# Sparse attention and expert layer on one core: routing moved on chip, tokens scattered straight from attention

## The chip, the cores and the metric

The kernel runs on one NeuronCore of a Trainium2 chip. The metric is device time in microseconds (us): 551.54 us for the kernel before (median of 3 runs, 551.34 to 552.23).

## The reference, cut to what matters

```
P = sinkhorn(sort_net)                       # 5 rounds, 8x8 per (batch, head)
k_sorted, v_sorted = P @ blocks(k), P @ blocks(v)      # blocks of 96 tokens
attn = softmax(q_blk @ k_sorted_blk.T / 8); x = attn @ v_sorted_blk   # B=4, H=8, S=768, D=64
x = x.transpose(0, 2, 1, 3).reshape(3072, 512)
logits = x @ w_gate + modality_bias[modality_id]       # 8 experts
e_idx = argmax(logits); gate_w = softmax(logits)[e_idx]
for e in range(8):                           # F = 1024
    out[e_idx == e] = gate_w * (relu(x[e_idx == e] @ w1[e]) @ w2[e])
```

Each token goes to one expert. The inputs are one fixed draw. x has a standard deviation of 0.0036, so the modality bias decides: modality 1 has its largest bias at expert 0 (0.722), modality 0 at expert 3 (0.643). The reference sends 1513 tokens to expert 0, 1559 to expert 3 and none to the others. In tiles of 128 tokens that is 12 + 13 = 25.

## The kernel before, in words

**Attention** (lines 113 to 342). k and v are sorted by matmuls with the block-diagonal P (`sort_k`, `sort_v`), batches 0 and 1 first (group 0), batches 2 and 3 (group 1) inside the loop. The loop has 32 units: unit u is one head h = u % 8 of half hf (four of the eight blocks) of two batches. A unit runs `scores` (PE), `expo` (ACT), `av` (PE, then a reciprocal and a multiply on DVE, L260 and L261) and, ahead, the next heads' query transposes (`prep_q`: a spread on DVE, six transposes on PE, a copy on DVE). The order up to line 343 is the order in which the code is written; each engine works its queue in order. POOL issues the loads of k, v, q and the weights on one DMA queue; these convert fp32 to bf16. After a head group ends, SP writes x to `x_scratch` in DRAM (L269).

**Gating** (L364 to L398): 24 tiles of 128 tokens are read back, transposed, multiplied by `w_gate`; one-hot, gate and rank within the tile stay on chip, and the counts go through DRAM.

**Placing** (L400 to L468): counts become expert bases, in matmuls of a few rows and four round trips through DRAM; then 24 indirect DMAs on POOL scatter (row number, gate) pairs to `sidx_scratch` (L465).

**Experts** (L474 to L515): 31 tiles, enough for any routing. Each loads its expert number into registers, its 128 indices (SP), gathers 128 rows of x (POOL, L481), transposes them (L487), runs the first layer (L493, 8 matmuls of 512 columns) with relu (L498, L500), transposes the result (L504, L505), runs the second layer (L508), scales (L512) and scatters 128 rows to the output (L513). All eight experts' weights lie in `w_all`, and the matmuls address it by register.

## Time and profile before

| stage of the profiled execution | from, us | to, us |
|---|---|---|
| first sort | 0 | 43.5 |
| 32 attention units | 43.5 | 122.7 |
| gating, first load of x to last count | 122.7 | 215 |
| bases and indices | 215 | 233.4 |
| 24 scatters of pairs | 233.4 | 332.8 |
| 31 expert tiles and the end | 332.8 | 553.4 |

The profiled execution took 555.13 us, with a span of 553.4 us from the first to the last instruction. Busy time over that span: PE 268.7 us (49%), DVE 199.5, POOL 153.7, ACT 143.7. HBM was read 59.83 MB. A span is read stage by stage: the engine that is busy on average need not be the one that a stage waits for.

### The profile page before, as it was taken

To read this page: it belongs to the slowest core of one execution; us is meant where nothing else is said; L and a number is where in the kernel's file an instruction comes from. 1 tells how busy PE (TensorE), PEld (TensorE's weight loads), DVE (VectorE), ACT (ScalarE), POOL (GpSimd) and SP (SyncE) were. 2 spreads that over 40 slices of the span, in tenths; PEclk is the share of its full clock that TensorE was granted. 3 is DMA by queue.
4 is the path that set the end of the run, shared out by engine and by line. 5 is a ranking of instruction groups with operands and counts; after the bars stand their busy time and mean duration, and the time that the engine had idled before them with its cause. 6 is when DMAs were issued, how large, how long until landed. Compare 5 with 4: busy or idle time off the path is not lost.

```text
span 553.4 us, 6871 instructions
## 1 busy us (share of the span) xinstructions
PE 268.7 (49%) x2044; PEld 153.5 (28%) x2044; DVE 199.5 (36%) x735; ACT 143.7 (26%) x445; POOL 153.7 (28%) x182
## 2 busy tenths in 40 slices
PE   0274696570233552000000004877887787887884
PEld 0264575440112331000000002333333333333331
DVE  7756456580233554100000001343344433433342
ACT  1142496240123552000000001333333323332331
POOL 9607414020101222222222222232232323323321
PEclk9999996555555555555555555999999989998998
DMA  6939999999994310000000001111111111111110
GB/s 129 210 62 157 66 216 222 222 221 235 224 227 81 59 43 1 8 0 0 0 0 0 0 0 29 49 57 59 58 58 55 58 58 58 64 53 58 31 22 1
DMA packets 40473, 43.56 MB, mean 79 GB/s; under 512 B 14300, under 2 KB 32773, under 8 KB 40182
## 3 DMA queue, kind: packets, MB, share of 16 engines
q0 software_dynamic: 24320, 36.72, 33.8%
q1 hardware_dynamic: 12662, 3.26, 3.6%
q10 hardware_dynamic: 3456, 3.15, 2.5%
q8 instruction: 18, 0.29, 0.2%
q14 instruction: 17, 0.14, 0.1%
HBM read 59.83 MB, written 11.33 MB: 129 GB/s over the span
## 4 chain that ended last, share of the span: by engine, by line
DMA 31%; PE 30%; issue 20%; DVE 12%; POOL 4%; ACT 2%; POOLq 0%; SPq 0%; ACTq 0%; DVEq 0%
DMA sidx_scratch<-rg_all,dest_i_all 14%; PE h_p L493 10%; PE y_p L508 9%; DMA q_in<-in_q_dram 4%; PE hT_p L504 4%; DVE y_sb L512 3%; DMA x_t<-x_scratch,idxg 3%; DMA out_dram<-y_sb,idxg 2%; POOL cnt_scratch L398 2%; DMA x_t<-x_scratch 2%; PE ka L185 2%; PE xT_p L487 1%; DMA v_sb<-in_k_dram 1%; PE va L193 1%; DVE w_all L261 1%
## 5 line engine op out<-in xcount | busy, mean ns | idle before, releaser
L487 PE MATMUL xT_p<-ident,x_t 128*128 128x128 bf16 x124 | 21.2, 221 | 139.8 <-DMA x_t<-x_scratch,idxg 121.9
L508 PE MATMUL y_p<-w_all,hT 128*128 x248 | 75.2, 376 | 0.0
L493 PE MATMUL h_p<-w_all,xT 128*128 x248 | 63.3, 401 | 8.9 <-issue 8.7
L481 POOL DMA_INDIRECT x_t<-x_scratch,idxg x31 | 30.1, 972 | 130.2 <-DMA idxg<-sidx_scratch 40.3
L488 ACT COPY xT<-xT_p 128x128 bf16<-128x128 bf16 x62 | 16.4, 265 | 165.8 <-PE xT_p L487 165.8
L504 PE MATMUL hT_p<-ident,h_sb 128*128 128x128 bf16 x248 | 49.4, 220 | 10.3 <-DVE hT L505 9.6
L488 DVE COPY xT<-xT_p 128x128 bf16<-128x128 bf16 x62 | 11.4, 217 | 109.7 <-PE xT_p L487 109.7
L487 PEld LDWEIGHTS <-x_t 128*128 128x128 bf16 x124 | 10.2, 97 | 141.9 <-DMA x_t<-x_scratch,idxg 124.3
L505 DVE COPY hT<-hT_p 128x128 bf16<-128x128 bf16 x124 | 27.9, 225 | 47.2 <-PE hT_p L504 44.5
L465 POOL DMA_INDIRECT sidx_scratch<-rg_all,dest_i_all x24 | 23.3, 973 | 77.1 <-DMA sidx_scratch<-rg_all,dest_i_all 72.9
L505 ACT COPY hT<-hT_p 128x128 bf16<-128x128 bf16 x124 | 32.7, 264 | 29.7 <-PE hT_p L504 26.9
L513 POOL DMA_INDIRECT out_dram<-y_sb,idxg x31 | 31.4, 1012 | 27.3 <-DVE xT L488 12.5
L498 DVE TENSOR_SCALAR h_sb<-h_p 128x512 bf16<-128x512 f32 x31 | 21.4, 692 | 48.4 <-PE h_p L493 46.8
L493 PEld LDWEIGHTS <-xT 128*128 128x128 bf16 x248 | 25.0, 101 | 47.6 <-issue 27.8
L508 PEld LDWEIGHTS <-hT 128*128 128x128 bf16 x248 | 23.8, 96 | 43.9 <-issue 15.7
L500 ACT ACTIVATE h_sb<-h_p 128x512 bf16<-128x512 f32 x31 | 18.5, 597 | 65.4 <-PE h_p L493 58.5
L371 PE MATMUL xT_p<-ident,x_t 128*128 128x128 bf16 x96 | 19.9, 278 | 27.5 <-ACT xT L372 14.6
L512 DVE TENSOR_SCALAR y_sb<-y_p,idxg 128x512 f32<-128x512 f32 x31 | 23.3, 751 | 27.2 <-PE y_p L508 27.2
L243 ACT ACTIVATE attnT<-sc 96x768 bf16<-96x768 f32 x32 | 26.2, 825 | 21.6 <-PE sc L237 21.6
L398 POOL DMA_DIRECT2D cnt_scratch<-cnt_sb x24 | 12.1, 504 | 58.0 <-ACT cnt_sb L397 41.0
L261 DVE TENSOR_TENSOR w_all<-op,rs 96x256 bf16<-96x256 f32 x64 | 26.9, 421 | 2.3
L504 PEld LDWEIGHTS <-h_sb 128*128 128x128 bf16 x248 | 20.6, 97 | 15.5 <-DVE h_sb L498 14.4
(128 smaller groups left out, 397.6 us busy)
## 6 DMA issues: line engine op xcount, KB each, us to landing
w_all<-in_moe_w_dram POOLq DMA_DIRECT2D x16, 1024.0 KB, 20.8
v_sb<-in_k_dram POOLq DMA_DIRECT2D x6, 512.0 KB
w_all<-in_v_dram POOLq DMA_DIRECT2D x2, 1536.0 KB, 14.6
q_in<-in_q_dram POOLq DMA_DIRECT2D x16, 192.0 KB, 13.0
x_scratch<-w_all SPq DMA_DIRECT2D x48, 64.0 KB, 5.7
x_t<-x_scratch ACTq DMA_DIRECT2D x24, 128.0 KB, 2.7
idxg<-sidx_scratch SPq DMA_DIRECT2D x31, 1.0 KB, 1.7
x_t<-x_scratch,idxg POOLq DMA_INDIRECT x31
```

The source lines that it names most:

```text
L243: nc.scalar.activation(attnT[u % 3][:, 0:8 * BLK].rearrange("p (r f) -> p r f", r=2), sc_tiles.pop(u)[0:BLK, :, 0:4 * BLK], ACT.Exp, scale ...
L261: nc.vector.tensor_tensor(xb[:, par, :, h], op[0:BLK, :, 0:D], rs.broadcast_to([BLK, 4, D]), ALU.mult)
L465: nc.gpsimd.indirect_dma_start(out=sidx_dram, out_offset=bass.IndirectOffsetOnAxis(ap=dest_i_all[:, t:t + 1], axis=0), in_=rg_all[:, t], i ...
L481: nc.gpsimd.indirect_dma_start(out=x_t, out_offset=None, in_=x_dram, in_offset=bass.IndirectOffsetOnAxis(ap=idx[:, :1], axis=0))
L487: nc.tensor.transpose(xT_p, x_t[:, c * 128:(c + 1) * 128], ident)
L488: (nc.scalar.copy if c % 2 else nc.vector.tensor_copy)(xT[:, c], xT_p)
L493: nc.tensor.matmul(h_p, xT[:, c], w_all[:, bass.ds(e_sv * WCOL + c * F + half * 512, 512)], start=(c == 0), stop=(c == 3))
L504: nc.tensor.transpose(hT_p, h_sb[:, fc * 128:(fc + 1) * 128], ident)
L505: (nc.scalar.copy if fc % 2 else nc.vector.tensor_copy)(hT[:, fc], hT_p)
L508: nc.tensor.matmul(y_p, hT[:, fc], w_all[:, bass.ds(e_sv * WCOL + 4 * F + fc * Dm, Dm)], start=(fc == 0), stop=(fc == 7))
L512: nc.vector.tensor_scalar(y_sb, y_p, gate_t[:, 0:1], None, ALU.mult)
L513: nc.gpsimd.indirect_dma_start(out=out, out_offset=bass.IndirectOffsetOnAxis(ap=idx[:, :1], axis=0), in_=y_sb, in_offset=None, bounds_chec ...
```

## The change

The tokens are handled in four quarters m of 768 (one half hf of one group, eight units). Each token gets a row of 516 bf16 in the attention buffer `xb`: 512 values, its token number and its gate.

- **Gating inside the attention loop.** While quarter m + 1 is in attention, quarter m is transposed from `xb` on PE (`gate_T`, eight 96x128 transposes, four times a quarter) and multiplied by `w_gate` (`gate_L`). `choose` makes the one-hot, `place` ranks the tokens with ten matmuls, the running counts staying on chip, and scatters eight blocks of 96 whole rows from `xb` into `xs_scratch`, which has a region of 3200 rows per expert. The fourth quarter's gating is done in tiles 0 to 6.
- **Weights only if used.** `load_w` reads a flag into a POOL register and issues the two halves of an expert's weights under that condition: experts 0 to 3 after quarter 0, all eight after quarter 2 and after quarter 3, each only if the expert is newly used. In this draw experts 0 and 3 are loaded in the first step; the other 18 calls have a false flag.
- **Tiles from tables.** After quarter 2 a table names expert and first row of 11 full tiles; after quarter 3 another does for the rest. A tile's rows come by a plain SP load at a register address, six buffers deep (`x_load`). 25 tiles always run; tiles 25 to 30 stand under conditions that are false in this draw. The tile loop is written as a pipeline: first layer of tile s, row transposes of s + 1, second layer of s - 1, hidden transposes of s, with one copy for four transposes. The scale moves from DVE to ACT. Zero rows are written behind each expert's last row (`pad_fill`).
- Gone are `x_scratch`, `sidx_scratch` and the passes of counts through DRAM, the filling of `sidx_scratch`, and the gathers. The modality numbers are loaded at the start in six DMAs of 4-byte elements.

```diff
-    for t in range(NT):
-        r0 = t * 128
-        x_t = mpool.tile([128, Dm], BF16)
-        nc.scalar.dma_start(out=x_t, in_=x_dram[r0:r0 + 128])
...
-        nc.gpsimd.dma_start(out=cnt_dram[t:t + 1], in_=cnt_sb)
...
-    for t in range(NT):
-        nc.gpsimd.indirect_dma_start(
-            out=sidx_dram,
-            out_offset=bass.IndirectOffsetOnAxis(ap=dest_i_all[:, t:t + 1], axis=0),
-            in_=rg_all[:, t], in_offset=None)
...
-    for s in range(NS):
-        e_sv = nc.values_load(slote_sb[0:1, s:s + 1], min_val=0, max_val=7)
-        idxg = mpool.tile([128, 2], I32)
-        nc.sync.dma_start(out=idxg, in_=sidx_dram[s * 128:(s + 1) * 128])
...
+    GW = Dm + 4
+    NTL = N // BLK
+    CAP = N + 128
+    S1, SU, SMAX = 11, 25, 31
...
+    xs_dram = nc.dram_tensor("xs_scratch", [E * CAP + 128, GW // 2], I32, kind="Internal").ap()
...
+    for e in range(1, E):
+        nc.gpsimd.memset(ebase[0:1, :, e:e + 1], float(CAP * e))
...
+    def gate_T(m, c):
+        tp = mipsum.tile([128, 8, BLK], BF16, tag="mi", name=f"gt{m}_{c}")
+        for t in range(8):
+            nc.tensor.transpose(tp[:, t], xb[m % 2][:, t, c * 128:(c + 1) * 128], ident[:BLK, :BLK])
+        (nc.scalar.copy if m == 2 else nc.vector.tensor_copy)(xTg_buf(m, c), tp)
...
+    def gate_L(m, c):
+        lg = mipsum.tile([BLK, 8, E], FP32, tag="mi", name=f"lg{m}_{c}")
+        for t in range(8):
+            nc.tensor.matmul(lg[:, t], xTg_buf(m, c)[:, t], wg_sb[:, c], start=True, stop=True)
...
+            nc.vector.tensor_tensor(la, la, lg, ALU.add)
...
+        mx = small.tile([BLK, 8, 1], FP32, tag="mx", name=f"mx{m}")
+        nc.vector.tensor_reduce(mx, la, AX.X, ALU.max)
+        ls = small.tile([BLK, 8, E], FP32, tag="ls", name=f"ls{m}")
+        nc.vector.tensor_tensor(ls, la, mx.broadcast_to([BLK, 8, E]), ALU.subtract)
+        key = small.tile([BLK, 8, E], FP32, tag="key", name=f"key{m}")
+        tw = bass.AP(tensor=tiew.tensor, offset=tiew.offset, ap=[tiew.ap[0], [0, 8], tiew.ap[1]])
+        nc.vector.scalar_tensor_tensor(key, ls, 0.0, tw, ALU.is_ge, ALU.mult)
...
+        nc.tensor.matmul(rkf, maskUT[0:BLK, :], oh.rearrange("p t e -> p (t e)"), start=True, stop=False,
+                         skip_group_check=True)
+        nc.tensor.matmul(rkf, ones_bf[0:BLK, :], ebase.rearrange("p t e -> p (t e)"), start=False, stop=False,
+                         skip_group_check=True)
+        nc.tensor.matmul(rk, ones_bf[0:BLK, :], pb, start=False, stop=False, skip_group_check=True)
+        for t in range(7):
+            ob = bass.AP(tensor=oh.tensor, offset=oh[:, t].offset, ap=[oh.ap[0], [0, 7 - t], [1, E]])
+            nc.tensor.matmul(rk[:, t + 1:8], ones_bf[0:BLK, :], ob, start=False, stop=(t == 6),
+                             skip_group_check=True)
...
+        nc.vector.tensor_tensor(sel_r, rk[0:BLK], oh, ALU.mult)
+        dest = small.tile([BLK, 8], I32, tag="dest", name=f"dest{m}")
...
+        scat[m] = []
+        for t in range(8):
+            nc.gpsimd.tensor_copy(icol[:, t:t + 1], idm[:, t // 4, t % 4:t % 4 + 1])
+            ins = nc.gpsimd.indirect_dma_start(
+                out=xs_dram, out_offset=bass.IndirectOffsetOnAxis(ap=dest[:, t:t + 1], axis=0),
+                in_=xt.bitcast(I32)[:, t], in_offset=None)
+            tc.declare_no_dep(ins.ins, group="xs", reason="scattered rows are disjoint")
+            tc.add_to_no_dep_group("xs", ins.ins)
+            scat[m].append(ins.ins)
...
+        nc.tensor.matmul(cp, ones_bf[0:BLK, :], ohs[(m + 1) % 2], start=True, stop=True)
...
+            nc.vector.scalar_tensor_tensor(fI, cnt[cm][0:1], 0.0, p, ALU.is_gt, ALU.subtract)
...
+    def load_w(st, e):
+        v_ = nc.values_load(flags[st][0:1, e:e + 1], engines=(PoolEng,), min_val=0, max_val=1)
+        w1v = w_all[:, e * WCOL:e * WCOL + 4 * F].rearrange("p (c f) -> p c f", c=4)
+        w2v = w_all[:, e * WCOL + 4 * F:(e + 1) * WCOL].rearrange("p (c f) -> p c f", c=8)
+        i1 = nc.gpsimd.dma_start(out=w1v, in_=moe_w1[e].rearrange("(c p) f -> p c f", p=128), cond=v_ > 0)
+        i2 = nc.gpsimd.dma_start(out=w2v, in_=moe_w2[e].rearrange("(c p) f -> p c f", p=128), cond=v_ > 0)
+        w_dma[st] += [i1.ins, i2.ins]
...
+    def pad_fill():
+        for e in range(E):
+            row = nc.values_load(prow[0:1, e:e + 1], engines=(SPEng,), min_val=0, max_val=E * CAP - 128)
+            ins = nc.sync.dma_start(out=xs_dram[bass.ds(row, 128)], in_=zrow.bitcast(I32))
...
+    def x_load(s, after=()):
+        tb, n = slot_tab(s)
+        row = nc.values_load(tb[0:1, 1, n:n + 1], engines=(SPEng,), min_val=0, max_val=E * CAP)
+        ins = nc.sync.dma_start(out=xt_b[s % XB].bitcast(I32), in_=xs_dram[bass.ds(row, 128)])
+        for a in after:
+            tc.add_manual_dep(ins.ins, a.name, SYNC, reason="rows of the slot")
...
+    def mX(s):
+        tp = mipsum.tile([128, 4, 128], BF16, tag="mi", name=f"mx{s}")
+        for c in range(4):
+            nc.tensor.transpose(tp[:, c], xt_b[s % XB][:, c * 128:(c + 1) * 128], ident)
+        nc.vector.tensor_copy(xT_b[s % 3], tp)
...
+    def mL1(s):
+        tb, n = slot_tab(s)
+        ev = nc.values_load(tb[0:1, 0, n:n + 1], engines=(PEng,), min_val=0, max_val=(E - 1) * WCOL)
+        hp = scpsum.tile([128, 2, 512], FP32, tag="sc", name=f"hp{s}")
+        for half in range(2):
+            for c in range(4):
+                w_mm(s, hp[:, half], xT_b[s % 3][:, c],
+                     w_all[:, bass.ds(ev + (c * F + half * 512), 512)], start=(c == 0), stop=(c == 3))
+            hd = h_b[s % 2][:, half * 512:(half + 1) * 512]
+            if half == 0:
+                nc.vector.tensor_scalar(hd, hp[:, half], 0.0, None, ALU.max)
+            else:
+                nc.scalar.activation(hd, hp[:, half], ACT.Relu)
+        st_["ev", s] = ev
...
+    def mH(s):
+        for z in range(2):
+            tp = mipsum.tile([128, 4, 128], BF16, tag="mi", name=f"ht{s}_{z}")
+            for c in range(4):
+                fc = z * 4 + c
+                nc.tensor.transpose(tp[:, c], h_b[s % 2][:, fc * 128:(fc + 1) * 128], ident)
+            (nc.scalar.copy if z else nc.vector.tensor_copy)(hT_b[s % 2][:, z * 4:(z + 1) * 4], tp)
...
+    def mL2(s):
+        ev = st_.pop(("ev", s))
+        yp = opsum.tile([128, Dm], FP32, tag="op", name=f"yp{s}")
+        for fc in range(8):
+            w_mm(s, yp, hT_b[s % 2][:, fc],
+                 w_all[:, bass.ds(ev + (4 * F + fc * Dm), Dm)], start=(fc == 0), stop=(fc == 7))
+        xt = xt_b[s % XB]
+        y = y_b[s % YB]
+        nc.scalar.activation(y, yp, ACT.Copy, scale=xt.bitcast(FP32)[:, Dm // 2 + 1:Dm // 2 + 2])
+        idc = xt.bitcast(I32)[:, Dm // 2:Dm // 2 + 1]
+        ix = small.tile([128, 1], I32, tag="ix", name=f"ix{s}", bufs=4)
...
+            nc.gpsimd.tensor_tensor(ix, idc, keep2[:, s - S1:s - S1 + 1], ALU.mult)
+            nc.gpsimd.tensor_tensor(ix, ix, pen2[:, s - S1:s - S1 + 1], ALU.add)
+        else:
+            nc.gpsimd.tensor_copy(ix, idc)
+        ins = nc.gpsimd.indirect_dma_start(
+            out=out, out_offset=bass.IndirectOffsetOnAxis(ap=ix, axis=0),
+            in_=y, in_offset=None, bounds_check=N - 1, oob_is_err=False)
...
+    for m in range(4):
+        for c in range(4):
+            at(8 * m + 2 * c + 2, gate_T, m, c)
+            at(8 * m + 2 * c + 3, gate_L, m, c)
+        if m < 3:
+            at(8 * m + 9, choose, m)
+            at(8 * m + 10, place, m)
+            if m == 0:
+                at(11, counts, 0)
+                at(11, make_flags, 1)
+                for e in range(EH):
+                    at(12, load_w, 1, e)
+            if m == 2:
+                at(27, counts, 2)
+                at(27, t1_a)
+                at(28, t1_b)
+                at(28, make_flags, 2)
+                at(29, t1_c)
+                for e in range(EH):
+                    at(29, load_w, 2, e)
...
+    nc.gpsimd.memset(zrow, 0.0)
+    nc.sync.dma_start(out=xs_dram[E * CAP:E * CAP + 128], in_=zrow.bitcast(I32))
+    for e in range(EH, E):
+        load_w(2, e)
+    for s in range(XB):
+        x_load(s, scat[0] + scat[1] + scat[2] if s == 0 else ())
...
+    def load3():
+        make_flags(3)
+        for e in range(E):
+            load_w(3, e)
...
+    hooks = {(0, 0): [(gate_T, (3, 3))], (1, 0): [(gate_L, (3, 3)), (choose, (3,))],
+             (1, 1): [(place, (3,))], (2, 0): [(counts, (3,))], (3, 0): [(t2_a, ()), (pad_table, ())], (5, 2): [(pad_fill, ())],
+             (4, 0): [(t2_b, ())], (5, 0): [(t2_c, ())], (6, 1): [(load3, ())]}
...
+    def run(sl, pre=()):
+        mX(sl[0])
+        for s in sl:
+            mL1(s)
+            for f, a in hooks.get((s, 0), []):
+                f(*a)
+            if s + 1 in sl:
+                mX(s + 1)
+            if s - 1 in sl:
+                mL2(s - 1)
+            for f, a in hooks.get((s, 1), []):
+                f(*a)
+            if s + XB - 1 < SU and s >= 1:
+                x_load(s + XB - 1, scat[3] if s + XB - 1 == S1 else ())
+            for f, a in hooks.get((s, 2), []):
+                f(*a)
+            mH(s)
+        mL2(sl[-1])
...
+    n2 = nc.values_load(nT2[0:1, 0:1], min_val=0, max_val=S2)
+    rest = ExitStack()
+    for s in range(SU, SMAX):
+        rest.enter_context(tc.If(n2 > s - S1))
```

The first place is POOL in units 8 to 16 of the attention loop, where weights and queries share POOL's queue. In the kernel before (`w_all<-in_moe_w_dram` is one half of an expert's weights, `q_in` the queries of two heads):

```order
L280 DMA w_all<-in_moe_w_dram 128x8x512
L278 DMA w_all<-in_moe_w_dram 128x4x1024
L102 DMA q_in_2_986<-in_q_dram 128x2x384 x2
L280 DMA w_all<-in_moe_w_dram 128x8x512
L102 DMA q_in_3_1027<-in_q_dram 128x2x384 x2
```

In the changed kernel (`ubuf<-in_q_dram` are queries, `xs_scratch<-xb` is a scattered row block, `fl` holds the flags; the pair of the first two rows stands eight times, the weight rows four times):

```order
L413 COPY xb_77<-idI 96x1
L414 DMA xs_scratch<-xb_77,dest_1084 25728x258
...
L448 TENSOR_LOAD fl_1162
L448 ISA x2
L451 ISA
L451 DMA w_all<-in_moe_w_dram 128x4x1024
L452 ISA
L452 DMA w_all<-in_moe_w_dram 128x8x512
...
L121 DMA ubuf<-in_q_dram 128x2x384 x4
```

The last query loads of the second group, which stood between single weight loads, now stand behind eight scatters and four pairs of weight loads.

The second place is SP between tiles 5 and 11 of the expert phase, the changed kernel alone (`prow` holds the ends of the experts' regions; before, SP had one plain load per tile there, `idxg<-sidx_scratch`). In brackets is what a row waits for; DMAHW with a number is one lane of SP's DMA completions:

```order
L577 TENSOR_LOAD prow [waits DVE_49]
L577 ISA x2
L578 ISA
L578 DMA xs_scratch<-v_sb_73 128x258 [waits DMAHW3_49,DMAHW4_49,DMAHW2_49,DMAHW7_49,DMAHW1_49,DMAHW0_49]
L577 TENSOR_LOAD prow
L577 ISA x2
L578 ISA
L578 DMA xs_scratch<-v_sb_73 128x258 [waits DMAHW5_49]
...
L585 TENSOR_LOAD tab_463 [waits DVE_49]
L585 ISA x2
L586 ISA
L586 DMA v_sb_73<-xs_scratch 128x258 [waits DMAHW4_49,Activation_49,Pool_49]
```

Eight writes of zero rows, each waiting for the one before it (the next lane), now stand ahead of the load of tile 11's rows.

The third place is PE inside one tile. Before, transposes of the hidden layer and the second layer's matmuls alternate:

```order
L504 LDWEIGHTS h_sb
L504 MATMUL hT_p<-ident,h_sb 128x128
L508 LDWEIGHTS hT
L508 ISA
L508 MATMUL y_p<-w_all,hT 128x512
L504 LDWEIGHTS h_sb
```

Now (`yp` is the second layer of the tile before, `ht` the transposed hidden layer of this tile, `hp` the first layer of the next):

```order
L599 MATMUL yp_2670<-w_all,ubuf 128x512
L625 LDWEIGHTS ubuf
L625 MATMUL ht_0_2696<-ident,ubuf 128x128
...
L625 MATMUL ht_1_2702<-ident,ubuf 128x128
L607 TENSOR_LOAD tab_462
L607 ISA x2
L599 LDWEIGHTS ubuf
L599 ISA
L599 MATMUL hp_2718<-w_all,ubuf 128x512
```

The eight second-layer matmuls now stand in a block between the first layer and the transposes that it feeds, so another tile's work lies between a result and its use.

599 lines of the change are left out of this document (323 added, 276 removed).

## The prediction, made before the result was known

> **What bounds the kernel now.** I read the granted clock over the 40 slices first, then the busy times stage by stage, then the chain of waits. Clock, in tenths of full speed:
>
> ```profile
> PEclk9999996555555555555555555999999989998998
> ```
>
> The stages (from:to and length in us; busy us and instructions of PE, PEld, DVE, ACT, POOL; granted clock; DMA share; GB/s):
>
> ```profile
> 0.00:43.50 43.50, 14.57 (x162) 12.69 (x162) 30.38 (x68) 10.79 (x20) 22.85 (x28) 1.00 0.66 128
> 43.50:122.70 79.20, 55.16 (x768) 44.96 (x768) 51.42 (x164) 39.20 (x60) 28.43 (x34) 0.78 1.18 188
> 122.70:145.40 22.70, 0.42 (x3) 0.26 (x4) 0.44 (x4) 0.18 (x1) 1.76 (x4) 0.50 1.17 231
> 145.40:233.40 88.00, 31.45 (x244) 18.74 (x243) 35.54 (x254) 28.95 (x147) 15.78 (x32) 0.50 0.44 82
> 233.40:332.80 99.40, 0.00 (x0) 0.00 (x0) 0.00 (x0) 0.00 (x0) 23.34 (x24) 0.50 0.01 0
> 332.80:543.40 210.60, 164.13 (x852) 75.55 (x852) 80.04 (x243) 63.02 (x212) 60.54 (x61) 0.96 0.16 50
> ```
>
> Between 122.7 and 332.8 us, 210 us, PE is busy for 32 us: that is the routing. The last 99 us hold nothing but 24 POOL instructions. The chain (start, length, what) says what they wait for, and shows one steady expert tile:
>
> ```profile
> 45.08 12.26 DMA q_in<-in_q_dram
> ...
> 93.15 12.38 DMA q_in<-in_q_dram
> ...
> 233.47 3.85 DMA sidx_scratch<-rg_all,dest_i_all
> ...
> 328.74 4.06 DMA sidx_scratch<-rg_all,dest_i_all
> ...
> 339.38 0.76 issue
> 340.14 3.57 PE h_p L493 x8
> ...
> 398.78 0.75 DVE y_sb L512
> ...
> 399.93 0.28 issue
> 400.21 1.89 PE h_p L493 x8
> 402.09 0.28 PE hT_p L504 x2
> ...
> 405.23 0.75 DVE y_sb L512
> ```
>
> Each scatter waits until the one before it has landed, about 4 us. The first layer of the first tile starts at 339.38 + 0.76 = 340.1. A tile takes 405.23 - 398.78 = 6.45 us. Attention waits for queries twice, 12 us each, because these share POOL's queue with other loads. Three stages therefore carry the change: attention (does it grow?), the way from its end to the first tile, and the tile's cadence.
>
> **The change part by part: attention.** An ACT exponential marks each unit; the five below are units 3, 10, 18, 22 and 31.
>
> ```profile
> 60.42 0.81 ACT L243 ACTIVATE attnT<-sc 96x768 bf16<-96x768 f32 x1
> 77.94 0.85 ACT L243 ACTIVATE attnT<-sc 96x768 bf16<-96x768 f32 x1
> 94.02 0.81 ACT L243 ACTIVATE attnT<-sc 96x768 bf16<-96x768 f32 x1 [1.80 <-PE sc L237]
> 108.12 0.81 ACT L243 ACTIVATE attnT<-sc 96x768 bf16<-96x768 f32 x1 [5.94 <-PE sc L237]
> 120.06 0.81 ACT L243 ACTIVATE attnT<-sc 96x768 bf16<-96x768 f32 x1 [0.44 <-PE sc L237]
> ```
>
> Prices of kinds of work (busy us, mean ns; what ended the idle time before):
>
> ```profile
> L221 DVE COPY w_all<-tq 128x768 bf16<-128x768 bf16 x16 | 8.9, 555 | 6.2 <-PE tq L218 6.1
> L260 DVE RECIPROCAL rs<-op 96x4 f32<-96x4 f32 x64 | 11.0, 172 | 11.0 <-PE op L257 10.7
> L261 DVE TENSOR_TENSOR w_all<-op,rs 96x256 bf16<-96x256 f32 x64 | 26.9, 421 | 2.3
> L382 DVE TENSOR_REDUCE stats<-logits 128x1 f32<-128x8 f32 x24 | 3.7, 154 | 0.2
> L451 DVE TENSOR_TENSOR tmp_all<-rank_all,basebc_all 128x192 f32<-128x192 f32 x1 | 0.4, 358 | 6.6 <-DMA basebc_all<-base_scratch 6.6
> L280 POOL DMA_DIRECT2D w_all<-in_moe_w_dram x8 | 7.2, 894 | 40.5 <-PE op L257 27.1 <-DMA modraw<-in_moe_modality_id_dram 13.4
> L328 POOL MEMSET v_sb<- 128x128 bf16 x1 | 0.7, 653 | 0.1
> L465 POOL DMA_INDIRECT sidx_scratch<-rg_all,dest_i_all x24 | 23.3, 973 | 77.1 <-DMA sidx_scratch<-rg_all,dest_i_all 72.9 <-DVE dest_i_all L458 4.2
> ```
>
> And the transfers (KB each, median us from issue to landing):
>
> ```profile
> w_all<-in_moe_w_dram POOLq DMA_DIRECT2D x16, 1024.0 KB, 20.8
> q_in<-in_q_dram POOLq DMA_DIRECT2D x16, 192.0 KB, 13.0
> x_scratch<-w_all SPq DMA_DIRECT2D x48, 64.0 KB, 5.7
> x_t<-x_scratch ACTq DMA_DIRECT2D x24, 128.0 KB, 2.7
> cnt_scratch<-cnt_sb POOLq DMA_DIRECT2D x24, 0.0 KB, 1.6
> ```
>
> Up to unit 3 I change nothing: the new iotas on POOL and the modality loads delay DVE by some us, but that unit waits for queries till 57.3 (first chain row) anyway. If they delayed those queries too, the cost would be the same few us. Units 3 to 10 took 77.94 - 60.42 = 17.5. Now the transposes and logits of quarter 0 stand among them, a DVE copy of 0.56 or a small add of 0.16 per unit; taken as 0.5 each, 3.5 in all (0 if DVE's gaps take them, 5 with PE's part on top). Unit 10 starts at about 81.5. There `place` adds about 2.5, then POOL issues eight scatters at 0.97 plus a small copy and gaps, 1.3 each: done at 94.5. No scatter waits for the landing of another now. Then four expert calls, two of them real: four halves at 0.9, four flag reads at 0.76 and two skipped issues, about 8.2, so POOL comes to the last four query loads at 102.7 (the kernel before: issued by 93). One MB half takes 1.05 MB / 0.22 = 4.7 us at the 219 to 231 GB/s of the rows, so the queries stand behind 4 x 4.7 = 18.8 us of weights begun at 96, plus 3.5 of their own: they land near 118.5. The unit that needs them, 18, was 16.1 after unit 10; with gating 22.5, it is ready at 104. **The wait** is 15 us (0 if transfers issued late overtake, 23 if the weights take their median 20.8 twice). Units 18 to 23 at 2.25 end near 132.
>
> Units 24 to 31: DVE has 16 pairs of L260 and L261 (9.5 us), three copies (1.7), and 40 small operations of quarters 2 and 3 and of the first table, 37 at 0.16 and three at 0.36 (7.0): 18.2 us, or 2.3 a unit. PE is cold there as before:
>
> ```profile
> 110.00:120.00 10.00, 9.48 (x131) 6.35 (x132) 9.03 (x33) 6.45 (x8) 1.64 (x2) 0.50 1.18 219
> ```
>
> These 10 us have PE busy for 9.48 and DVE for 9.03, at 1.33 us a unit ((120.06 - 108.12) / 9), and the clock stays at 0.50. With gating matmuls on that PE I take 2.6 a unit, 21 us, and 2 for the end: **attention ends near 155** instead of 122.7 (bounds 137, no wait and 1.9 a unit, and 165). The Trainium skill, page "TensorE: Matmul & The Clock Gate", section "What's actually happening", says that some 3.4 us of sustained activity bring the full clock; this row has three times that at half clock. By the rule these units would be bound by DVE alone, 2.3 each, 2.4 us less in all.
>
> **From attention to the first tile.** The last scatter of quarter 2 leaves POOL at about 152. Four skipped expert calls follow. No row shows a skipped load. Its lower bound is one exposed register load with its issue, 0.76 (the row at 339.38); the upper adds two full DMA issues, 0.76 + 2 x 0.89 = 2.5. I take 1.6, the middle: 158.4. Then POOL clears the zero rows (0.7), SP writes them (1.6 to 5.7; 2.3 taken, as the queue is empty by then) and loads tile 0 (2.7), whose transposes and copy follow in 0.8 (L504 below, L221): 164.9. The other four skipped calls run beside this until 165. First layer at **165**, against 340.1: 175 us come from here. What is late next is only quarter 3, which the tiles hide.
>
> **The tiles.** Durations of a first-layer matmul and of a hidden transpose:
>
> ```profile
> L493 PE MATMUL h_p<-w_all,xT 128*128 x248 | 63.3, 401 | 8.9 <-issue 8.7
> L504 PE MATMUL hT_p<-ident,h_sb 128*128 128x128 bf16 x248 | 49.4, 220 | 10.3 <-DVE hT L505 9.6 <-DVE h_sb L498 0.3 <-issue 0.3
> ```
>
> Eight in 1.89, the last lasting 0.40, start (1.89 - 0.40) / 7 = 0.213 apart; two transposes in 0.28 start 0.06 apart. Before, the y copy (0.75), the transposes between copies and the register load stood in the chain of every tile. Now each result has eight other matmuls before its use. A tile is 16 x 0.213 = 3.4, plus 12 transposes at 0.06 to 0.12 (0.09: 1.1), plus 0.28 for the register load, which PE still does in order: 4.85. The bounds are 4.1 (nothing but PE's stream) and 6.45 (the chain stays). The Trainium skill, page "DMA: Bandwidth & Descriptors", section "Latency and other measured facts", gives a register load a floor of about 0.6 us; by that the tile would be 5.2 and the sum 8 more. 25 x 4.85 = 121. On top: gating and tables of quarter 3 on PE and DVE in tiles 0 to 6, 7 (0 to 12); cold clock in the first tile, where eight matmuls took 3.57 in the chain instead of 1.89, and its first bubble, 5. The eight zero-row writes on SP are serial at 1.6 to 5.7; at 2.4 they take 19 us, and six row buffers at 4.85 give tile 11's load about 23: no wait. The eight skipped calls in tile 6 take POOL 13; an output waits for them, but four y buffers last for 19 us. Without that cover it is 13. PE ends at 165 + 121 + 12 = 298.
>
> **The end.** Before:
>
> ```profile
> 546.68 0.75 DVE L512 TENSOR_SCALAR y_sb<-y_p,idxg 128x512 f32<-128x512 f32 x1 [0.88 <-PE y_p L508]
> ```
>
> From its end, 547.43, to the span's end, 553.4, are 6.0 us. Now ACT scales in 0.6, POOL forms the index in two small steps before issuing, and the branch over tiles 25 to 30 follows (0 to 4): 9.5. The span is 307.5; the span before was 553.4 for a median of 551.54, so **306 us**.
>
> **The rivals.**
> - *The tile keeps its chain* (6.45): some wait, in the psum buffers or the copies of four transposes, takes the old ones' place. For it speaks that PE is busy for 164.13 of 210.60 us in the stage's row, 5.3 a tile, so that the order can take 1.2 a tile at most by closing gaps and has to get the rest from work side by side; against it the order itself, eight matmuls ahead of each use. 25 x 1.6 = 40 more: 346.
> - *Routing is hidden entirely*: queries are not late and attention ends at 137; first layer at 147, tiles at 4.5: 147 + 113 + 12 + 9.5 = 281, 280 as a median. Against it stand the two 12 us waits for queries in the chain.
> - *The zero-row writes bind*: at 5.7 each they hold SP for 46 us against 23 of cover. Tile 11 waits about 24 to 26: 331.
> - *The skipped loads are not skipped.* The change would not do what it says: at 9.4 us an expert, 2 + 8 + 8 more experts cost 19 before the late queries, 75 before the first tile and 53 of 75 behind the tiles: 453. Slower than before follows if such a call costs over (551.5 - 306) / 18 = 13.6 us, between 9.4 (streaming) and two halves at the median 20.8; then it is above 552.
>
> **How the numbers follow.** Forecast 0.60 (its own range 283 to 331, from attention's end -18 to +10, the skipped calls at 0.76 to 2.5, the tile at 4.5 to 5.4); old cadence 0.13; hidden routing 0.15; writes 0.07; loads not skipped 0.04, of which half is slower; 0.01 for no change by accident. The range goes from 274 (hidden routing with tiles at 4.3) to 346 (old cadence). About 0.2% either way is what a measurement here can tell from no change; all cases but half of the fourth rival lie far below: faster 0.97, same 0.01, slower 0.02.
>
> **What would show it.** In the changed profile: query loads issued near 103 landing near 118, a wait of PE on them before unit 18, and the clock at 0.5 in units 24 to 31; first L1 matmul at 150 to 175; skipped loads as POOL time of 1 to 2.5 us without bytes; the start of first layers 4.85 apart in tiles 12 to 24, PE over 90% busy there; x loads on SP early. Wrong would be a first layer after 185, a cadence over 5.6, HBM traffic of more than two experts' weights, or a tile 11 that waits for SP.

## The result and the profile after

| | before | after |
|---|---|---|
| median of 4 runs each, us | 551.44 (550.22 to 552.23) | 320.46 (319.70 to 321.26) |
| ratio, 95% interval | | 0.581 (0.579 to 0.583) |
| span of the profiled execution, us | 553.4 | 318.3 |
| bytes moved by POOL's DMA queue, MB | 36.72 | 23.11 |

The forecast was 306 us, its range 274 to 346. The stages of the changed kernel (columns as for the kernel before; the rows: start of attention, units 3 to 18, the wait for queries, units 19 to 31, the way to the first tile, tiles 0 to 6, the rest of the tiles, the end):

```profile
43.50:64.60 21.10, 9.08 (x116) 7.70 (x118) 15.62 (x34) 3.39 (x6) 11.52 (x33) 1.00 0.69 113
64.60:113.30 48.70, 43.65 (x565) 37.55 (x561) 30.56 (x105) 25.50 (x45) 17.18 (x30) 1.00 0.40 70
113.30:132.20 18.90, 2.78 (x40) 2.49 (x40) 3.93 (x18) 1.51 (x4) 2.34 (x4) 1.00 1.01 172
132.20:161.60 29.40, 24.75 (x325) 19.84 (x321) 23.50 (x98) 12.24 (x18) 17.88 (x31) 1.00 0.18 52
161.60:173.20 11.60, 1.06 (x10) 0.71 (x10) 1.59 (x7) 0.00 (x0) 1.42 (x18) 1.00 0.17 49
173.20:208.00 34.80, 28.56 (x188) 15.16 (x188) 17.41 (x65) 9.73 (x17) 13.66 (x24) 1.00 0.27 83
208.00:303.60 95.60, 80.71 (x524) 41.74 (x523) 28.92 (x58) 33.02 (x57) 25.85 (x67) 1.00 0.25 85
303.60:318.30 14.70, 2.30 (x16) 1.01 (x13) 0.42 (x1) 1.85 (x3) 2.38 (x4) 0.70 0.07 23
```

The 210 us of routing with an almost idle PE are gone. Attention is 39 us longer (122.7 to 161.6), 19 of them in one stretch with PE busy for 2.8. The timeline names what is waited for (start, length, engine, instruction, idle time before it and its releaser):

```profile
112.16 0.70 POOL L121 DMA_DIRECT2D ubuf<-in_q_dram  x1 [3.99 <-DVE w_all L296]
116.94 2.14 POOL L121 DMA_DIRECT2D ubuf<-in_q_dram  x3 [4.09 <-DMA w_all<-in_moe_w_dram]
128.73 0.63 DVE L128 COPY w_all<-ubuf 128x768 bf16<-128x768 bf16 x2 [14.05 <-DMA ubuf<-in_q_dram]
...
161.62 0.04 POOL L451 DMA_DIRECT2D w_all<-in_moe_w_dram  x1
163.13 0.04 POOL L451 DMA_DIRECT2D w_all<-in_moe_w_dram  x1 [1.12 <-DMA w_all<-in_moe_w_dram]
...
164.56 0.04 POOL L451 DMA_DIRECT2D w_all<-in_moe_w_dram  x1 [0.97 <-DMA w_all<-in_moe_w_dram]
...
172.46 0.04 POOL L452 DMA_DIRECT2D w_all<-in_moe_w_dram  x1 [0.45 <-DMA w_all<-in_moe_w_dram]
```

Three of the four last query loads could not even be issued until some weights had drained, and DVE waited 14 us for them. The skipped loads take 0.04 us of work a half, but a call with its flag read and its two conditions takes 164.56 - 163.13 = 1.43 us of POOL, and the last of the eight ends at 172.5. One steady tile, in the chain of waits:

```profile
243.44 0.88 PE hp L599 x4
244.34 0.70 DVE ubuf L615
245.09 1.02 PE hp L599 x4
246.11 0.22 PE mx L593 x4
246.33 1.73 PE yp L599 x8
248.06 0.45 PE ht L625 x8
248.51 0.88 PE hp L599 x4
```

The tile is 248.51 - 243.44 = 5.07 us. A DVE relu stands in the middle of PE's eight first-layer matmuls: both halves lie in one tile of psum, the memory that matmuls write to; the relu of half 0 is written ahead of the matmuls of half 1, and these wait until it has read. Over 25 tiles PE's waits on L615 are 19.6 us.

**Two rows that mislead.** On the page, the queue's line (packets, MB, share) says less than before, 36.72, and the memory line more, 59.83:

```profile
q0 software_dynamic: 12704, 23.11, 33.5%
...
HBM read 106.11 MB, written 10.91 MB: 368 GB/s over the span
```

The 40 weight halves written in the program are 84 MB of fp32, the four that ran 8.4. The line counts the skipped ones; the queue's bytes do not: in the run without the eight calls after quarter 2 (below) the line says 72.55, which is 33.56 or 16 halves less, and the queue still 23.11. And the clock column says 1.00 throughout attention, but the matmuls say otherwise. Eight score matmuls, twice in the kernel before and once in the changed one:

```profile
72.55 0.50 PE L237 MATMUL sc<-w_all 64*128 64x96 bf16 x8
74.39 0.34 PE L237 MATMUL sc<-w_all 64*128 64x96 bf16 x8
```

```profile
81.21 0.50 PE L308 MATMUL sc<-ubuf,w_all 64*128 64x96 bf16 x8
```

In the kernel before they take 0.34 us from 74 to 88 us and 0.50 elsewhere, also from 110 to 120, where its column says 0.50. In the changed kernel they take 0.50 in every unit, so PE is at half clock all through attention, whatever the column says. The same holds for the first tile: four first-layer matmuls of 1.87 us at 173.17, 0.88 and 1.02 later.

One sentence on the change needs a correction: three of the four gating passes of a quarter run within its own eight units, as its heads are finished; only the last pass, the choice and the placing run in the next quarter's.

### The profile page after: what moved, and what is told of

Read it like the earlier page. It is cut to its first block, busy times and chain, and to the rows that moved or that the text cites. A ratio compares the mean times of both kernels' runs of the same rounds, so it can differ in the third digit from the quotient of the medians.

```text
span 318.3 us, 5924 instructions
## 1 busy us (share of the span) xinstructions
PE 207.5 (65%) x1929; PEld 138.9 (44%) x1929; DVE 152.3 (48%) x442; ACT 98.0 (31%) x163; POOL 113.3 (36%) x237
## 3 DMA queue, kind: packets, MB, share of 16 engines
q0 software_dynamic: 12704, 23.11, 33.5%
## 5 line engine op out<-in xcount | busy, mean ns | idle before, releaser
L599 PE MATMUL hp<-w_all,ubuf 128*128 x200 | 52.9, 388 | 21.4 <-DVE ubuf L615 19.6
L599 PEld LDWEIGHTS <-ubuf 128*128 128x128 bf16 x400 | 37.4, 98 | 63.1 <-issue 29.4
L644 POOL DMA_INDIRECT out_dram<-v_sb,ix x25 | 24.7, 990 | 80.3 <-ACT ubuf L626 55.6
L599 PE MATMUL yp<-w_all,ubuf 128*128 x200 | 47.2, 379 | 0.4 <-DVE ubuf L626 0.4
L414 POOL DMA_INDIRECT xs_scratch<-xb,dest x32 | 30.2, 943 | 41.5 <-issue 20.4
L329 DVE TENSOR_TENSOR xb<-op,rs 96x256 bf16<-96x256 f32 x64 | 26.9, 421 | 2.2
L626 DVE COPY ubuf<-ht 128x512 bf16<-128x512 bf16 x25 | 10.6, 425 | 34.6 <-PE ht L625 34.6
L615 DVE TENSOR_SCALAR ubuf<-hp 128x512 bf16<-128x512 f32 x25 | 17.3, 693 | 19.2 <-PE hp L599 19.2
L325 PE MATMUL op<-v_sb,attnT 96*128 96x65 bf16 x256 | 20.7, 245 | 0.1
L213 PEld LDWEIGHTS <-w_all 128*128 128x128 bf16 x192 | 11.5, 129 | 19.3 <-issue 18.7
L325 PEld LDWEIGHTS <-attnT 96*128 96x128 bf16 x256 | 17.4, 134 | 0.6 <-DVE xb L329 0.6
L221 PEld LDWEIGHTS <-w_all 128*128 128x128 bf16 x128 | 14.2, 181 | 6.3 <-issue 5.8
```

The source lines that it names most:

```text
L221: nc.tensor.matmul(acc[:, z], v_cols[:, ch * 4 + z], bd_v[g], start=True, stop=True)
L325: nc.tensor.matmul(op[:, j], attnT[u % 2][:, c0:c0 + 128], v_sb[g][0:BLK, par * 64 + h * 8 + i, 0:D + 1], start=True, stop=True)
L329: nc.vector.tensor_tensor(xt[:, par * 4:(par + 1) * 4, h * D:(h + 1) * D], op[0:BLK, :, 0:D], rs.broadcast_to([BLK, 4, D]), ALU.mult)
L414: ins = nc.gpsimd.indirect_dma_start(out=xs_dram, out_offset=bass.IndirectOffsetOnAxis(ap=dest[:, t:t + 1], axis=0), in_=xt.bitcast(I32)[: ...
L599: ins = nc.tensor.matmul(*a, **kw).ins
L615: nc.vector.tensor_scalar(hd, hp[:, half], 0.0, None, ALU.max)
```

## The experiments

Ratios are to the kernel before on the same chip; the changed kernel's is 0.581. A hundredth is 5.5 us. The changed kernel itself was not run again beside the experiments, where the kernel before took up to 0.7% longer than 551.44 in the runs with a ratio, so a difference of ratios can be some 2 us off; where the medians say less, both are given.

**The relus behind both halves.**

```diff
-            hd = h_b[s % 2][:, half * 512:(half + 1) * 512]
-            if half == 0:
-                nc.vector.tensor_scalar(hd, hp[:, half], 0.0, None, ALU.max)
-            else:
-                nc.scalar.activation(hd, hp[:, half], ACT.Relu)
+        nc.vector.tensor_scalar(h_b[s % 2][:, 0:512], hp[:, 0], 0.0, None, ALU.max)
+        nc.scalar.activation(h_b[s % 2][:, 512:1024], hp[:, 1], ACT.Relu)
```

> The edit: the two relus of a tile are written after all eight first-layer matmuls, and not after four each. In the profile of the changed kernel the second four matmuls of every tile wait 0.78 us for the relu of the first half on DVE (19.6 us over 25 tiles); both halves lie in one psum tile. Theory 'the wait is an order of the code: half 1 is held back until half 0 has been read': it goes, a tile takes 5.07 - 0.78 = 4.3 us, and the time falls by about 19 us to 301. Rival 'PE's stream sets the tile and the wait only moves': now DVE starts its relu later, the transposes of the hidden layer wait for it instead, and the cadence stays within 0.2 us of 5.07: 317 to 320.

0.5577 (0.5548 to 0.5606), 13 us less (12 by the medians, 308.9 for 320.5). The chain over two tiles, and SP and PE in the timeline:

```profile
236.45 1.75 PE hp L599 x8
...
244.75 1.75 PE hp L599 x8
```

```profile
208.87 16.46 SPq L578 DMA_DIRECT2D xs_scratch<-v_sb  x8
229.76 0.40 PE L593 MATMUL mx<-ident,v_sb 128*128 128x128 bf16 x4 [3.29 <-DMA v_sb<-xs_scratch]
```

The wait came from the order in the code: two tiles now take 244.75 - 236.45 = 8.30, one 4.15. (Whether two psum tiles instead of one would do the same was not tried.) That is more than the 0.78 expected, and yet the time fell by less: six buffers of 4.15 us no longer cover the eight serial zero-row writes, and PE stands 3.3 us before tile 11. This is the mechanism of the prediction's third rival, at a price of 2.06 us a write. The first tiles kept their gaps: in three of them PE waits, up to 2.0 us, for a DVE copy that stands behind the small operations for quarter 3's tables.

**The same, with the zero-row writes declared disjoint.**

```diff
             ins = nc.sync.dma_start(out=xs_dram[bass.ds(row, 128)], in_=zrow.bitcast(I32))
+            tc.declare_no_dep(ins.ins, group="pad", reason="each expert has rows of its own")
+            tc.add_to_no_dep_group("pad", ins.ins)
```

> The edit: both relus behind all eight first-layer matmuls, and the eight zero-row writes declared disjoint of each other. With the first alone a tile took 4.15 us instead of 5.07, and then PE stood 3.3 us before tile 11, since its rows' load stood on SP behind eight serial writes of 2.06 us each. Theory 'the write chain is what took back a part': the writes take under 8 us in all instead of 16.5, the 3.3 us go, and the time is 3 to 4 below that run, 0.5577 - 0.006 = 0.551 of before (306 on its scale of 555). Rival 'the load itself is late for another reason' (its buffer comes free late, or SP's loads wait for landings): the ratio stays at 0.557.

0.5497 (0.5474 to 0.5519), 4 us below the run before. The eight writes:

```profile
209.40 8.47 SPq L578 DMA_DIRECT2D xs_scratch<-v_sb  x8
```

So it was the chain of writes that took a part back; a write is 1.06 us of SP now.

**The weights behind the queries.**

```diff
-                    at(12, load_w, 1, e)
+                    at(16, load_w, 1, e)
```

> The edit: the four conditional expert loads after quarter 0 are written at unit 16 instead of unit 12, so behind the last four query loads on POOL's queue. Theory of the prediction 'units behind 18 wait for queries that stand behind 4 MB of weights': the wait of 14 us for queries (18 us without an exponential) shrinks to under 5, attention ends 12 to 17 us earlier and the time falls by about 14 to 306. Rival 'the queries are late by themselves' (they are issued only when the buffers are free, and took 13 us to land before): the wait keeps 10 us or more and the time stays within 4 us. A second rival: the eight scatters of quarter 1, now behind the weights' issues, become late and give it back, 318 or more.

0.5681 (0.5642 to 0.5719), 7 us less by the ratio, 4 by the medians (316.3 for 320.5), and not 14. Units 19 and 20 come at 118.0 instead of 132.2: the long wait was queries behind weights. But unit 24, the first to write quarter 1's buffer again, is held for 6.94 and 1.08 us, since the scatters are late, as the second rival had named (POOL, then DVE):

```profile
127.03 0.95 POOL L414 DMA_INDIRECT xs_scratch<-xb,dest  x1 [5.04 <-DMA w_all<-in_moe_w_dram]
```

```profile
138.07 0.42 DVE L329 TENSOR_TENSOR xb<-op,rs 96x256 bf16<-96x256 f32 x1 [6.94 <-DMA xs_scratch<-xb,dest]
```

Quarter 1's scatters now stood behind the weights, and quarter 3 may not overwrite their buffer before they have been read. The first tile starts 6.7 us earlier, at 166.5, but a part is lost again at tile 11, whose rows are loaded behind the zero-row writes:

```profile
226.60 0.61 PE L593 MATMUL mx<-ident,v_sb 128*128 128x128 bf16 x4 [1.68 <-DMA v_sb<-xs_scratch]
```

**The weights behind quarter 1's scatters as well.**

```diff
-                    at(12, load_w, 1, e)
+                    at(19, load_w, 1, e)
```

> The edit: the four conditional expert loads after quarter 0 are written at unit 19, behind the last queries and behind the eight scatters of quarter 1. With the loads at unit 16 the wait for queries went from 14 to under 4 us, but two scatters of quarter 1 then stood 7 us behind the weights on POOL, and unit 24 waited 8 us for its buffer. Theory 'POOL's queue is full while 4 MB drain, and whatever comes next waits': now neither queries nor quarter 1 wait, attention ends before 148, but the scatters of quarter 2 (ready at about 135) wait until about 146 and the first tile starts at 166 to 170: 313 to 317, a ratio of 0.567 to 0.574, hardly better than the loads at unit 16 (0.568). Rival 'only queries and the buffer counted': the scatters of quarter 2 do not wait, the first tile starts at 157 to 160 and the ratio is 0.550 to 0.557.

0.5727 (0.5686 to 0.5767), as the theory had it. The last exponential is at 143.6 instead of 158.7, 15 us earlier, and then:

```profile
144.68 0.94 POOL L414 DMA_INDIRECT xs_scratch<-xb,dest  x1 [5.31 <-DMA w_all<-in_moe_w_dram]
```

The scatters of quarter 2 wait behind the weights, and the first tile starts at 167.4. In all three places where 4 MB were put on POOL's queue in one piece, what came next waited.

**Four experts loaded, not two.**

```diff
+        kw = {} if st == 1 else {"cond": v_ > 0}
-        ... cond=v_ > 0)
+        ... **kw)
```

> The edit: the loads after quarter 0 lose their condition, so that experts 0 to 3 are loaded (8 halves) and not only 0 and 3 (4 halves); the other flags stay. Theory 'the queries behind unit 18 wait for the weights ahead of them on the queue': 4 more halves at 4.7 us are 19 us, less 3 of skipped calls, that the wait grows by; 335 to 341. Rival 'the queries' own issue or the buffers set that wait': 324 or less.

One run: 335.1 us, a span of 333.3, 15 over the changed kernel's. The wait for queries grew by 20 (waits: us in total, times, the longest), and the first tile starts 20 later. Between the last output's issue and the span's end lie 3.7 us here, and 9.5 to 9.8 in the changed kernel and its ten other variants, so that 5.8 come back; why was not found:

```profile
DVE w_all L128 <- DMA ubuf<-in_q_dram: 34.0, 1, 34.0
```

**No calls after quarter 2.** The eight calls whose flags are false in this draw are left out.

```diff
-                    at(29, load_w, 2, e)
+                    pass
-    for e in range(EH, E):
-        load_w(2, e)
```

> The edit: the eight conditional expert loads after quarter 2 are left out; their flags are all false in this draw, so no byte less is moved. They stand on POOL from 161.6 to 172.5 us, 1.42 us each, and the clearing of the zero rows and the first rows' load stand behind the first four. Theory 'a skipped call costs POOL 1.4 us, and four or more of them are on the way to the first tile': the first first-layer matmul comes 5 to 7 us earlier than 173.2 and the time falls by 5 to 7. Rival 'the landing of the last scattered rows sets the first load anyway': the first tile moves by under 2 us.

0.5714 (0.5693 to 0.5735), 5.5 us less by the ratio, 3.7 by the medians (316.8 for 320.5). The first layer starts at 169.5 instead of 173.2, 3.7 earlier and not 5 to 7: three DMAs in a row then set it, the last scatter until it has landed (2.4 us), the zero rows' write that waits for it (2.1) and the load of tile 0's rows (2.1).

**One gating pass of four.**

```diff
         for c in range(4):
-            at(8 * m + 2 * c + 2, gate_T, m, c)
-            at(8 * m + 2 * c + 3, gate_L, m, c)
+            if c == 0 or m == 3:
+                at(8 * m + 2 * c + 2, gate_T, m, c)
+                at(8 * m + 2 * c + 3, gate_L, m, c)
```

> The edit: of the four gating passes (eight transposes, a copy, eight matmuls, an add) of quarters 0 to 2 only the first is kept, so three quarters of the products x times w_gate are missing from the logits of those tokens; the routing goes by the bias alone and keeps its counts. Theory 'gating keeps PE at half clock in the second sort': the kernel before had one stretch of 3.4 us with PE busy for all of it (70.8 to 74.2), and from there to 88 us eight score matmuls took 0.34 us; in the changed kernel, with small waits in every such stretch, they take 0.50 throughout. Without the passes the uninterrupted stretch is back, scores fall to 0.34 in units 8 to 14, and attention ends 12 to 20 us earlier. Rival 'gating costs only its own work': nine passes at 1.3 to 1.5 us of PE, 10 to 13 us, scores at 0.50 throughout. Rival 'hidden': under 4 us.

0.5657 (0.5639 to 0.5674), 9 us less by the ratio, 6 by the medians (314.2 for 320.5). From unit 3 to unit 16 it takes 34.6 us instead of 42.6. The scores:

```profile
80.04 0.34 PE L308 MATMUL sc<-ubuf,w_all 64*128 64x96 bf16 x8
...
85.57 0.50 PE L308 MATMUL sc<-ubuf,w_all 64*128 64x96 bf16 x8
```

The full clock comes back for some three units and is lost again. So the theory holds for a few units at most, and most of the 8 us seems to be the rival's, the work of the passes itself; the two were not separated. Unit 18 comes 8.7 us earlier, but the queries land only 4.2 earlier, at 124.5 instead of 128.7, so the wait takes 4.5 back, and the last exponential is 5.6 us earlier. And a gapless stretch is not all that it takes. Two stretches of the kernel before and of this one (PE's busy time comes first after the length):

```profile
70.10:76.80 6.70, 6.70 (x117) 5.94 (x114) 4.27 (x16) 6.24 (x11) 1.66 (x2) 1.00 1.24 207
```

```profile
87.10:92.30 5.20, 5.20 (x72) 4.64 (x70) 2.58 (x11) 4.57 (x9) 4.22 (x8) 0.50 0.23 67
```

In the first, 6.7 us without a gap, the scores fall to 0.34; in the second, 5.2 us, they stay at 0.50, although PE is busy for 7.48 of the 7.50 us around it, from 84.9 to 92.4.

**Fillers on PE.**

```diff
+    def filler():
+        fp = mipsum.tile([128, 512], FP32, tag="mi", name="fill")
+        for _ in range(16):
+            nc.tensor.matmul(fp, ident, ubuf[:, 0:512], start=True, stop=True)
+    at(12, filler)
```

> The edit: at unit 12 of attention PE gets 16 more matmuls of 512 columns that nobody reads. In the changed kernel eight score matmuls take 0.50 us in every unit, while the clock row says 1.00 from 40 us on; the same matmuls took 0.34 in units 7 to 14 of the kernel before, which followed the one stretch of 3.4 us without a gap of PE. Theory 'PE is at half clock and gets the full one after some 3.4 us without a gap': the first 8 fillers start 0.43 us apart, the last 0.21, and the scores of the next unit or two take 0.34, until a gap. Rival 'the score matmuls are slower for another reason (their operands, the gating between them)': the fillers are 0.21 apart from the first, or 0.43 to the last, and the scores stay at 0.50. The time says little: the 5 us stand ahead of the wait for queries of 18; 316 to 325.

One run: 333.9 us, a span of 332.1, 14 over. PE's timeline, and three stretches:

```profile
93.89 4.16 PE L653 MATMUL fill<-ubuf,ident 128*128 128x512 bf16 x16
101.67 0.39 PE L308 MATMUL sc<-ubuf,w_all 64*128 64x96 bf16 x8
104.45 0.50 PE L308 MATMUL sc<-ubuf,w_all 64*128 64x96 bf16 x8
```

```profile
90.00:96.00 6.00, 6.00 (x61) 4.29 (x61) 2.81 (x12) 3.16 (x5) 4.71 (x9) 1.00 0.20 55
98.00:102.00 4.00, 1.88 (x33) 1.61 (x31) 0.59 (x2) 0.18 (x1) 2.77 (x6) 0.98 0.26 74
102.00:106.00 4.00, 2.72 (x36) 2.55 (x35) 2.89 (x11) 3.38 (x6) 1.54 (x6) 0.50 0.75 100
```

Sixteen matmuls in 4.16 us are 0.25 apart, between 0.43 and 0.21: the clock rose among them, sooner than after eight. Then PE is busy for 1.88 of 4 us, the scores go from 0.39 to 0.50, and the column drops to 0.50, for durations that the changed kernel's column called 1.00. So the cause is PE's clock, and not the score matmuls. The time was missed by 9 us. Against the changed kernel the first tile starts 2.7 us later and the tiles take 11 more: two of them instead of one run at half clock at the start, and in the fifth DVE stands still from 202.0 to 207.4 us, PE behind it for 5.25. The trace names that wait's releaser only as "remote"; why both came about is open.

**Scatters that wait for each other.**

```diff
-            tc.declare_no_dep(ins.ins, group="xs", reason="scattered rows are disjoint")
-            tc.add_to_no_dep_group("xs", ins.ins)
```

> The edit: the declaration that scattered rows are disjoint is taken off the 32 scatters of row blocks, one part of the change undone. Theory 'without it each scatter waits for the landing of the one before, as in the kernel before (4.1 us instead of 1.43 each)': quarter 0 takes 21 us longer and pushes weights and queries back, quarter 1 holds up the attention buffer that unit 24 writes, quarter 2 holds up the first tile by another 21: 360 to 385. Rival 'attention hides the scatters of quarters 0 and 1': only quarter 2 counts, about 342.

One run: 369.1 us, a span of 367.1, 49 over. Waits:

```profile
DVE w_all L128 <- DMA ubuf<-in_q_dram: 21.2, 1, 21.2
DVE xb L329 <- DMA xs_scratch<-xb,dest: 17.4, 2, 12.3
PE mx L591 <- DMA v_sb<-xs_scratch: 33.9, 2, 23.8
```

A scatter now takes about 3.2 us, not 4.1. All three stages named pay: attention ends 21 us later (180.0 for 158.7), the first tile starts 35 later, PE waiting 23.8 us for its rows, and a later tile waits another 10.

**Free scatters in the kernel before.** The 24 scatters of pairs get the same declaration, alone.

> The edit: the kernel before, with the 24 scatters of (row, gate) pairs declared disjoint and nothing else changed: one part of the change alone. Theory 'the 99 us were landings that each scatter waited for': a scatter takes 1.0 to 1.4 us, the stage 25 to 34 us, and the time falls by 62 to 72, to about 485 on the scale of 551. Rival 'the pairs take the time to be written, 128 packets of 8 bytes at a time': the landings pile up and the stage stays over 80 us, 535 or more.

One run: 490.8 us beside 557.6, 67 less. The first and the last of the 24:

```profile
235.68 1.04 POOL L465 DMA_INDIRECT sidx_scratch<-rg_all,dest_i_all  x1 [4.45 <-DVE dest_i_all L458]
...
265.10 0.97 POOL L465 DMA_INDIRECT sidx_scratch<-rg_all,dest_i_all  x1 [0.30 <-issue]
```

They start 1.28 us apart, so most of the 99 us were landings. In the kernel before, two added lines alone gain 67 us, where the whole change gains 231.

**Tile by tile.**

```diff
-        mX(sl[0])
         for s in sl:
+            mX(s)
             mL1(s)
...
-            if s + 1 in sl:
-                mX(s + 1)
-            if s - 1 in sl:
-                mL2(s - 1)
...
             mH(s)
-        mL2(sl[-1])
+            mL2(s)
```

> The edit: the tile loop is written tile by tile (row transposes, first layer, hidden transposes, second layer of one tile), one part of the change undone; copies of four transposes, scale on ACT and all else stay. Theory 'another tile's work hides the copies': now row copy 0.42, relu wait 0.78, second relu 0.6, hidden copy 0.5 and the scheduling gaps stand in the tile: 5.07 + 1.9 = 7.0 us, 25 times: about 366 (355 to 372). Rival 'the copies of four are the gain, not the order': 6.0 or less, under 343. Rival 'PE's stream alone': 5.1 to 5.3, under 327.

One run: 362.4 us, a span of 360.6, 42 over. PE's timeline over a tile:

```profile
263.21 1.02 PE L599 MATMUL hp<-w_all,ubuf 128*128 x4 [0.60 <-DVE ubuf L594]
...
266.77 0.40 PE L625 MATMUL ht<-ident,ubuf 128*128 128x128 bf16 x4 [0.52 <-ACT ubuf L617]
...
269.83 1.02 PE L599 MATMUL hp<-w_all,ubuf 128*128 x4 [0.60 <-DVE ubuf L594]
```

A tile takes 269.83 - 263.21 = 6.62. The waits for the row copy and the second relu are back, beside the one for the relu of half 0: the order of the loop is worth 1.55 us a tile.

**A version that is faster than both.** The relu order and the free zero-row writes as above; the loads of experts 0 and 1 stay at unit 12, those of 2 and 3 go to unit 19; the spare zero rows are written at unit 17.

```diff
-                    at(12, load_w, 1, e)
+                    at(12 if e < 2 else 19, load_w, 1, e)
```

> The edit: relus behind all eight matmuls, zero-row writes disjoint, the loads of experts 0 and 1 after quarter 0 left at unit 12 and those of 2 and 3 moved to unit 19 (so 2 MB ahead of the last queries and 2 MB behind quarter 1's scatters), and the clearing and writing of the spare zero rows moved from the end of attention to unit 17. Theory: 17 us from the tiles as before, and a wait for queries of about 5 instead of 14, none for the buffer, scatters of quarter 2 at most 4 us late, first tile at 161 to 164 instead of 173: 320.5 - 17 - 10 = 293 (288 to 299), a ratio of 0.525 to 0.543. Rival 'the gains overlap': POOL's scatters and skipped calls fix the first tile at 170 or later, 300 to 304.

293.5 us (292.4 to 294.5), 0.5305 (0.5281 to 0.5329): 27 to 28 us below the changed kernel. The first layer:

```profile
163.10 3.33 PE L601 MATMUL hp<-w_all,ubuf 128*128 x8 [6.13 <-DMA w_all<-in_moe_w_dram]
```

It starts 10 us earlier, and what ends its wait of 6.13 us is the last of the eight skipped calls; this version was not tried without them. In this draw each piece of weights is 2 MB because the two used experts fall one into each half.

## Why the prediction was right

The direction, the size and the chain of stages held; the span came out 11 us over the 307.5 of the sum. By its own terms:

- *Start of attention, 60.4 forecast, 64.6 measured.* Nothing was to change since the unit waits for queries anyway. That wait went, but the spreading of k (copies into the layout for the sort), which it had covered, was in the way, with POOL and DVE copying side by side:

```profile
54.62 3.74 POOL L112 COPY w_all<-v_sb 64x2048 bf16<-64x2048 bf16 x2
```

```profile
55.10 3.80 DVE L112 COPY w_all<-v_sb 64x2048 bf16<-64x2048 bf16 x1
60.38 0.68 DVE L112 COPY w_all<-v_sb 64x2048 bf16<-64x2048 bf16 x1
```

  The same DVE copy takes 0.68 us alone and 3.80 here. A cover that goes shows what lay under it. No run took the two copies apart.
- *Units 3 to 10, 21 forecast, 23.2 measured; 10 to 18, 22.5 and 25.4.* The step that failed is the basis: it took the units' time before, 17.5, which was partly at full clock, and added 0.5 for gating. In the changed kernel's attention the full clock never came.
- *The wait for queries, 15 forecast, 18.9 measured (from unit 18's exponential to the next), and its cause confirmed by three runs.* It began 9 us later than forecast because the units did. The queries landed at 128.7 instead of 118.5: the first weights were issued at 101.7 and not at 96, and from 105 to 128 us the DMAs moved 205 GB/s, where the forecast took 219 to 231. The 3.4 us from the landing to the next exponential were not in the sum. The query loads were taken as issued near 103; they were issued at 112 and 117, since POOL was held while weights drained. That held the queries up no further, as the transfers went on without a pause. The two rows of 12 us that the forecast read as waits in the kernel before are transfers from issue to landing; PE stood still for 6.8 and 4.8 us there.
- *Units 19 to 31, 29 us for the 36 forecast.* 2.25 and 2.6 a unit were too much. The three slips of attention, 13 us, less these 7 leave its end at 161.6 instead of 155: sizes that missed both ways, and partly cancelled, inside the bounds of 137 and 165.
- *To the first tile, 10 forecast, 11.6 measured.* A skipped call was put at 1.6, between 0.76 and 2.5, and took 1.43; the zero rows' write and the load took 2.3 and 2.2. The last skipped call ends at 172.5, just ahead of the first layer at 173.2.
- *The tiles, 133 forecast and 133 measured, by other terms.* The terms of a tile add up to 4.8 and not 4.85. The register load (0.28) no longer shows, and transposes cost 0.67 and not 1.1; that is 0.7 less. Against it stand matmuls of 3.63 for 3.4, and the wait of 0.78 for the relu, which the order of rows could have told and the prediction did not look for: 5.07. The extras were 6 us, not 12. The sum was right by chance.
- *The end, 9.5 forecast, 12 from PE's last matmul.* Of the 12, 9.5 lie behind the last output's issue. The kernel before has 4.7 there, and the run with four experts 3.7, so it need not be so long; whether branch or landing makes the difference was not found.

The rivals: the old cadence did not come back (5.07, and 6.62 when the order is undone); routing was not hidden entirely, since the queries were late; the zero-row writes bound nothing in the changed kernel, though only just (the load of tile 11's rows starts at 228.4 and takes about 2.2, and PE uses them at 230.75), cost 0.4 to 1.7 us in four variants with the same 5.07 a tile, and 3.3 at 4.15; the loads were skipped, as the queue's 23.11 MB and the 1.43 us a call show. The sign of a failure given for that, memory traffic, would have misled. PE was to be busy for over 90% of the later tiles and was for 84% (80.71 of 95.60 us), for the relu's wait. The clock in units 24 to 31 was at half, by durations; read from the column, that point would have been called wrong.

The forecast set the row of 110 to 120 us, 9.48 of 10 busy at half clock, against a rule. The runs leave it so: in attention 6.7 us without a gap brought the full clock, 5.2 us did not, and the changed kernel's first tiles got it with gaps:

```profile
175.10:182.00 6.90, 4.95 (x29) 2.96 (x29) 2.67 (x5) 1.18 (x2) 0.00 (x0) 1.00 0.14 38
```

PE is busy for 4.95 of 6.90 us there, with first-layer matmuls of 512 columns, and these go from 1.87 for four to 1.04. The Trainium skill, page "TensorE: Matmul & The Clock Gate", section "What's actually happening", asks for some 3.4 us of sustained activity, in a window that runs freely; a window that a stretch need not fill would fit the 5.2 us, though hardly the 7.48 of 7.50 around them, and not the first tile, if busy is what the profile counts. The full clock is lost at nearly the same share of busy time: in the kernel before PE is busy for 4.72 of the 6.80 us from 84.2 to 91.0, with no gap over 1.14, and the scores go from 0.34 to 0.50. What is counted stays open.

## What to carry to other kernels

Look for what one queue has to do in order: here weights, queries and scattered rows share POOL, and each place for 4 MB of weights moved the wait to whatever came next, while two pieces of 2 MB in two gaps left a wait of 4.6 us for the queries instead of 14. When a stage becomes shorter, work that it covered comes up, as the zero-row writes did at 4.15 us a tile and the spreading of k at the start. And write matmuls that share a psum tile ahead of its first reader: a relu between two halves cost 0.78 to 0.92 us a tile.

## What was not expected of the hardware

A call of two DMAs under a false condition cost its engine 1.43 us, flag read included, about a tenth of what would have made the change a loss, and the profile's memory line counts its bytes all the same. The clock column stood at 1.00 while score matmuls took 0.50 us instead of 0.34; durations of one and the same instruction are the surer sign. PE was busy for 5.2 us without a gap and stayed at half clock, and left it within 6.9 us that it was busy for 72% of; what decides was not found.
